# Output and mean-square matmuls of batches 1 to 7 on four quadrants of the TensorE array, with the order of work retuned

## The chip, the core and the metric

One core of a Trainium2 chip. The metric is device microseconds of one execution. Executions vary here by several per cent: a run counts as slow when it is over 1.5% above the fastest of its kernel, and fast runs are compared with fast runs. All positions in time below come from profiled executions. The two kernels were profiled in fast runs (192.91 us before).

## The reference

Linear attention without a mask, a root-mean-square norm per head, then a mixture of experts in which each of the 8 batches goes to one expert as a whole:

```python
kv  = einsum('bhsd,bhse->bhde', k, v)              # 8 batches, 8 heads, 576 tokens, 64 per head
out = einsum('bhsd,bhde->bhse', q, kv)
x   = out / sqrt(mean(out*out, -1) + 1e-6) * g_norm     # heads side by side: 576 x 512
e   = argmax(x.mean(tokens) @ w_gate)              # one of 8 experts for a batch
y   = softmax_prob[e] * relu(x @ w1[e]) @ w2[e]    # 512 -> 1024 -> 512
```

A batch's expert is known only when its attention is done, so the load of its weights can only be issued after its gate.

## The kernel before

The whole program is one list of steps, `ORDER`. A step is the batch, a letter, a number, and `x` where the eviction goes to the other of the two eviction engines:

```python
# L load q/k/v   T transpose q   K  k^T v of all heads   O  kv^T q (a pair of heads)
# M mean square  X normalise     G  gate: 0 sums, 1 matmul + index, 2 exp on GpSimd, 3 value
# W load the expert's weights (0: w1, 1: w2)   D warm-up matmuls
# m expert units: 0-7 blocks of layer 1, 9-16 halves of layer 2, 8 the last 64 tokens
ORDER = ( ... "2Q0x 0D1 0G2x 1K0 2T0x 1O0 1O2 1M0 0G3 0m0 2T2 1O1 0m3x 3L0x 3L1 1M1 1X0x 1O3 0m4 "
  "0m5 1X1 1M2 1M3x 0m1 1X2 0m7 1X3x 1G0 3L2x 2T3x 2K0x 0m2 1G1 2O0 0m6x 1G2 2T1x 2O2 " ... )
```

Each engine works through its own part of the list in order. The parts that the argument touches:

```python
def s_o(b, c, h=None, x=False):                    # one pair of heads
    po = ... psum("a")                             # tag "a": two buffers for all attention steps
    for i in range(2):                             # two halves of 288 tokens, whole array
        nc.tensor.matmul(po[:, i, 0:HS], kvb[:, b % 2, c, :],   # kv of 2 heads, block-diagonal 128x128
                         s["qT"][:, c, i * HS:(i + 1) * HS], start=True, stop=True)
    nc.scalar.activation(part(s["sq", c], h), po, AF.Square)
    if b > 0:
        copy(x, o, po)                             # one 128x576 copy frees the buffer
def s_m(b, c, h=None):                             # the same with `ones`, block-diagonal 1/64
    ...
    nc.scalar.activation(part(s["rs", c], h), pm[...], AF.Abs_reciprocal_sqrt, bias=epsc)
def s_index(b, pg):                                # G1: the expert's index into a register of GpSimd
    evs.append(nc.values_load(ixs[0:1, b, 0:1], engines=(mybir.EngineType.Pool,), ...))
def s_w(b, i):                                     # old weights are first copied to this batch's slot
    nc.vector.tensor_copy(W[:, own, ...], W[:, ds(sv, 1), ...])
    nc.gpsimd.dma_start(W[:, own, :, fs], (moe_w1, moe_w2)[i][ds(ev, 1), :, fs] ..., cond=cond)
def load_qkv(b, ...):                              # all loads of q, k and v are issued by GpSimd too
    nc.gpsimd.dma_start(t[0:R, hs], src[b, hs]...)
```

GpSimd's instruction stream thus holds the load of q, k and v of later batches, the register load of each gate, the exponentials, and the weight loads: whatever waits there holds all that is listed behind it (a wait of 14.6 us below shows it).

Of the kernel before, what the change touches and what calls it, by code (L numbers as in the profile page):

```python
# [11 lines left out]
F32 = mybir.dt.float32  # L12
F16 = mybir.dt.float16
# [8 lines left out]



ORDER = (
    "0R1 0R2 0R0x 0K0x 0T0 0C0 0K1 0T1x 0O0x 2L0x 0C1 0D1 0O1x 0M0x 0K2x 0X0 0T2 0M1 0C2x "
    "0D1 0D1 0O2x 0T3 0X1x 0C3 0K3 0M2x 1T0 0O30x 0O31 0M30 2L2x 0D1 0D1 0D1 0X2 0M31 0D1 "
    "0X30 0D1 0D1 0X31x 0G1x 0W0x 2L1x 0P0x 0D1 1T1 1T2 1T3 0D1 0D1 0D1 0D1 0D1 0W1 0D1 "
    "2Q0x 0D1 0G2x 1K0 2T0x 1O0 1O2 1M0 0G3 0m0 2T2 1O1 0m3x 3L0x 3L1 1M1 1X0x 1O3 0m4 "
    "0m5 1X1 1M2 1M3x 0m1 1X2 0m7 1X3x 1G0 3L2x 2T3x 2K0x 0m2 1G1 2O0 0m6x 1G2 2T1x 2O2 "  # L30
    "4L0x 2O1 0m9 4L1 1G3x 2M0 0m10x 4L2x 3Q0 2M1x 0m8x 2X0 5L0x 2O3x 0m15 2M2x 0m13 2X1x "
    "1W0 2X2x 3T0x 0m14 5L2x 5L1x 2M3 3T1x 0m16x 2X3x 3K0 3T2x 2G0 0m11 3T3 3O0 1W1x "
    "0m12x 3O2 1m0 1m7 2G1x 1m2 2G2x 3M0x 4Q0 1m5 3X0x 4T0 1m1 3O1 2W0 1m6 1m4x 3M2x 1m3 "
    "3M1x 4K0x 2W1 1m11 4T1 6L0x 3O3x 2G3 1m9x 1m12 3X1x 4T3x 3X2 3M3 1m10x 4T2 1m13 4O0x "
    "1m15 4O2 1m16 4M0 3X3x 1m14x 3G0x 4O1x 5K0x 1m8 4M1 4X0 2m0 4O3 2m7 3G1x 2m4 5Q0 2m3 "
    "6L1x 2m5 5T0 4M3 3W0x 2m1 2m2 3G2x 4X1x 2m6 4M2 5T3 3G3 4X2 2m13x 2m14x 5T1 4X3x "
    "5O0x 2m9x 6L2x 3W1 2m10x 2m15x 2m16x 5O1 2m8x 4G0 5T2x 6Q0 5M0x 2m11x 2m12x 4G1 3m0 "
    "6T0x 7L0x 3m5 6T1x 4W0 3m7x 3m6 5X0x 6T2x 5M1 3m3x 3m4 5O3 4G2x 3m1x 4G3 6T3x 7L1 "
    "5X1x 3m2 5O2 6K0 3m8x 5M2x 3m13 5M3 3m11x 3m14x 5X2x 4W1x 5X3x 3m12 6O0 5G0x 7Q0 "
    "3m9x 3m10x 3m15 6M0 3m16x 7L2 4m0x 6O1x 4m1x 7T0x 4m2x 5G1x 7T2x 5G2x 4m7 4m5x 6O2 "  # L40
    "4m4 5W0x 6X0x 4m3 6O3 5G3 5W1x 4m6 6M2x 4m9x 4m10x 4m11x 6M1x 6M3x 4m12x 6X1x 6X2x "
    "7T1 4m8 7K0 6X3x 4m15 4m16 4m13x 7O0x 6G0 4m14 6G1x 5m0 5m4x 6W0 6G2x 5m7 7T3x 5m6 "
    "5m1x 7M0x 5m3 5m2 7X0x 5m5x 6G3x 7O1x 5m11 7O2 5m12x 6W1 5m15x 7M2x 5m16x 7M1 5m8 "
    "5m13x 7O3 5m9x 5m14x 7X1 5m10 7M3x 6m0 6m2 6m5 7X2x 6m3 7X3x 7G0x 7G1 6m6 6m7 6m1 "
    "6m4 7G2x 7G3x 6m11 7W0 6m12x 6m13x 6m14 6m9 6m10x 6m15 6m16 6m8 7m0 7m5 7m6 7W1x 7m2 "
    "7m3 7m1 7m7 7m4 7m13x 7m14x 7m15 7m16 7m11 7m12x 7m9x 7m10x 7m8x "
)


# [1 line left out]
def kernel(  # L51
# [11 lines left out]
    nc = tc.nc  # L63
# [16 lines left out]
    att = ctx.enter_context(tc.tile_pool(name="att", bufs=2))  # L80
    sm = ctx.enter_context(tc.tile_pool(name="sm", bufs=3))
    xp = ctx.enter_context(tc.tile_pool(name="xp", bufs=3))
    hp = ctx.enter_context(tc.tile_pool(name="hp", bufs=1))
    outp = ctx.enter_context(tc.tile_pool(name="outp", bufs=5))
    ps0 = tc.tile_pool(name="ps0", bufs=1, space=bass.MemoryType.PSUM)
    psp = [ps0.__enter__()]
# [42 lines left out]
    nc.vector.memset(ones, 0.0)  # L129
    nc.vector.memset(ones[0:64, 0:64], 1.0 / Dh)  # L130
    nc.vector.memset(ones[64:128, 64:128], 1.0 / Dh)
    epsc = const.tile([P, 1], F32)
    nc.vector.memset(epsc, EPS)
    mean = const.tile([P, P], F32)
# [17 lines left out]
    def s_qt(b, c, x=False):  # L152
        s = st[b]
        if "qT" not in s:
            s["qT"] = att.tile([P, NP, S], F16, tag="qT", name="qT")
        p32 = psum("t", 1, 1) if first[0] else psum("a")
        pt = p32.bitcast(F16)
        for j in range(NJ):
            if "qr" in s:
                nc.tensor.transpose(pt[:, 0, j * R:(j + 1) * R], s["qr"][0:R, c, j],  # L160
                                    ident[0:R, 0:R])
                continue
            for i in range(2):
                nc.tensor.transpose(pt[64 * i:64 * i + 64, 0, j * R:(j + 1) * R],
                                    kvq[b][0][0:R, 2 * c + i, j, :], ident[0:R, 0:R])
        s["pt", c] = pt
        if b > 0:
            s_tc(b, c, x)
# [15 lines left out]
    def s_kv(b, prs):  # L184
        kt, vt = kvq[b][1:3]
        kv = kvb[:, b % 2]
        p32 = psum("kv", 1, 1) if first[0] else psum("a")
        pk = p32[:, 0].rearrange("p (c e) -> p c e", c=NP)
        for c in prs:
            for j in range(NJ):  # L190
                for i in range(2):
                    nc.tensor.matmul(pk[64 * i:64 * i + 64, c, 64 * i:64 * i + 64],  # L192
                                     kt[0:R, 2 * c + i, j, :], vt[0:R, 2 * c + i, j, :],
                                     start=(j == 0), stop=(j == NJ - 1))
        cs = slice(prs[0], prs[-1] + 1)
        nc.vector.tensor_copy(kv[0:64, cs, 0:64], pk[0:64, cs, 0:64])
        nc.vector.tensor_copy(kv[64:128, cs, 64:128], pk[64:128, cs, 64:128])


    def part(t, h):  # L200
        return two(t) if h is None else two(t)[:, h:h + 1]

    def s_o(b, c, h=None, x=False):
        s = st[b]
        po = (psum("p", 1) if h == 1 else psum("m")) if first[0] else psum("a")
        for i in range(2) if h is None else (h,):
            nc.tensor.matmul(po[:, i, 0:HS], kvb[:, b % 2, c, :],  # L207
                             s["qT"][:, c, i * HS:(i + 1) * HS], start=True, stop=True)
        po = po[:, :, 0:HS] if h is None else po[:, h:h + 1, 0:HS]
        if not h:  # L210
            s["sq", c] = sm.tile([P, S], F16, tag="sq", name="sq")
        nc.scalar.activation(part(s["sq", c], h), po, AF.Square)  # L212
        if b > 0:
            o = two(sm.tile([P, S], F32, tag="o", name="o"))
            copy(x, o, po)
            po = o
        s["o", c, h] = po

    def s_m(b, c, h=None):
        s = st[b]  # L220
        pm = (psum("p", 1) if h is None else psum("tkv"[h:2 * h + 1], 1, 1)) if first[0] \
            else psum("a")
        for i in range(2) if h is None else (h,):
            nc.tensor.matmul(pm[:, i if h is None else 0, 0:HS], ones,  # L224
                             s["sq", c][:, i * HS:(i + 1) * HS], start=True, stop=True)
        if not h:
            s["rs", c] = sm.tile([P, S], F32, tag="rs", name="rs")
        nc.scalar.activation(part(s["rs", c], h), pm[:, 0:2 if h is None else 1, 0:HS],  # L228
                             AF.Abs_reciprocal_sqrt, bias=epsc)

    def s_x(b, c, h=None):
        s = st[b]
# [16 lines left out]

    def s_row():  # L250
        s = st[0]
        pg = psum("t", 1, 1)[0:1, 0, 0:E]
        for c in range(NP + 1):
            nc.tensor.matmul(pg, s["pl"][:, c:c + 1], wg[:, min(c, NP - 1)], start=(c == 0),
                             stop=(c == NP))
        s["pg"] = pg
        s_index(0, pg)

    def s_index(b, pg):
        n = pg.shape[0]  # L260
        mx = sm.tile([P, 8], F32, tag="mx", name="mx")
        nc.vector.max(mx[0:n], pg)
        nc.vector.max_index(ixs[0:n, b], mx[0:n], pg)
        evs.append(nc.values_load(
            ixs[0:1, b, 0:1], engines=(mybir.EngineType.Pool,), min_val=0, max_val=E - 1,
            skip_runtime_bounds_check_because="it is the index of the largest of E values"))
        return mx

    def s_dl(b, mx, pg):
# [32 lines left out]
    def s_w(b, i):  # L302
# [2 lines left out]
        cond = None  # L305
        if b > 0:
            if b > 1 and i == 0:
                st[b]["sv"] = nc.values_load(
                    st[b]["src"][0:1, 0:1], engines=(mybir.EngineType.DVE,), min_val=0,
                    max_val=NW - 1,  # L310
                    skip_runtime_bounds_check_because="it is one of two numbers of slots")
            sv = st[b].get("sv", 0)
            for h in range(2):
                n = W.shape[2] // 2
# [53 lines left out]
    def m_2(b, t, fcs, x=False):  # L368
# [7 lines left out]
        if t == 4:  # L376
# [6 lines left out]
            if last:  # L383
                ot = outp.tile([P, D // 2], F32, tag="ot4", name="ot4")
                scaled(x, ot, po[:, 0, 0:D // 2], b)
                for i in range(2):
                    eng = nc.scalar if i and b == B - 1 else nc.sync
                    eng.dma_start(ob[NJ - 1, R - 64:R, i * D // 2:(i + 1) * D // 2],
                                  ot[64 * i:64 * i + 64])
            return  # L390
        for fc in fcs:
            nc.tensor.matmul(po[:, 0, :], s["hT"][:, fc, t * P:(t + 1) * P], w2[:, fc, :],  # L392
# [28 lines left out]
    def emit(tok):  # L421
# [6 lines left out]
        if f == "m":  # L428
            unit(b, c, x)
        elif f == "D":  # L430
            warm(psum("kv", 1, 1) if first[0] else psum("a"), c)
        elif f == "R":
            cast_first(c)
        elif f == "P":
# [6 lines left out]
        elif f == "K":  # L441
            s_kv(b, [c] if b == 0 else range(NP))
        elif f == "C":
            s_tc(b, c)
        elif f == "G":
            if (b, c) == (0, 1):
                s_row()
# [2 lines left out]
        elif f == "Q":  # L450
            s_qr(b)
        elif f == "W":
            s_w(b, c)
        elif f == "L":
            load_qkv(b, 1, only=(c,))
        elif f == "T":
            s_qt(b, c, x)
        elif f == "O":
            s_o(b, c, h, x)
        else:  # L460
            dict(M=s_m, X=s_x)[f](b, c, h)

    for tok in ORDER.split():
        emit(tok)
# [30 lines left out]
```

## Time and profile before

| | before |
|---|---|
| median of 3 runs | 193.95 us (193.09 to 199.57) |
| TensorE busy | 170.8 us of a span of 191.0 |
| VectorE, ScalarE busy | 110.8 and 106.6 us |
| gate matmuls of batches 1, 2, 7 | 40.9, 58.0, 158.9 us |
| TensorE's last matmul ends | 187.05 us |

The page's main lines are in the prediction. Two more views are needed to compare with later. The first cuts TensorE's time into three stretches: from batch 1's k-v product to batch 2's gate, from there to batch 7's gate, and from there to TensorE's end. The columns of a table of stretches are the stretch, its length, then busy us and number of instructions of each engine, the mean clock granted to TensorE, the DMA share and GB/s.

```profile
26.75:58.00 31.25, 28.39 (x361) 20.07 (x361) 24.33 (x60) 22.35 (x36) 12.42 (x16) 1.00 1.30 213
58.00:158.90 100.90, 99.15 (x951) 67.81 (x951) 67.96 (x173) 64.02 (x101) 23.13 (x21) 1.00 1.17 218
158.90:187.05 28.15, 28.14 (x196) 17.00 (x194) 6.49 (x16) 11.90 (x18) 1.79 (x4) 1.00 0.37 95
```

TensorE is idle 2.9, 1.8 and 0.0 us in the three. The second view is TensorE's timeline of batch 1's attention, the first stretch of the kernel in which it has little else to do (start, length, line, operation, idle before it and who ended that):

```profile
26.75 0.95 PE L192 MATMUL ps_a<-vt,kt 96*64 96x64 f16 x48
...
28.66 0.82 PE L207 MATMUL ps_a<-qT,kvb 128*128 128x288 f16 x4 [0.35 <-DVE kvb L197]
30.61 0.40 PE L224 MATMUL ps_a<-sq,ones 128*128 128x288 f16 x2 [1.13 <-DVE o L179]
30.85 1.14 PE L352 MATMUL ps_m<-xT,W 128*128 128x288 f16 x8
...
40.94 0.28 PE L283 MATMUL ps_a<-ts,mean 128*128 128x8 f32 x2
```

From the product to the gate matmul it takes 14.19 us. The wait of 1.13 us for a copy is the longest; single pairs alternate with whole blocks of batch 0's layer 1 (L352).

### The profile page before, as it was taken

How to read it: one execution, taken by the hardware profiler on the slowest of the kernel's cores; microseconds unless marked ns; L12 is line 12 of the kernel's file. 1: busy time of each engine (PE TensorE's matmuls, PEld its weight loads, DVE VectorE, ACT ScalarE, POOL GpSimd, SP SyncE). 2: the span in 40 equal slices, each digit the busy share in tenths (PEclk: the TensorE clock that was granted, in tenths of full speed). 3: DMA queues.
4: the chain of work that ended last, by engine and by line, in shares of the span. 5: the costliest groups of instructions: out<-in, count | busy, mean ns of one | idle time of the engine just before them, and what ended most of it. 6: DMA issues, size and time to landing. Idle time of an engine off the chain costs nothing.

```text
span 191.0 us, 4338 instructions
## 1 busy us (share of the span) xinstructions
PE 170.8 (89%) x1691; PEld 113.0 (59%) x1691; DVE 110.8 (58%) x289; ACT 106.6 (56%) x168; POOL 50.4 (26%) x64
## 2 busy tenths in 40 slices
PE   0297787998999999899999999999999999999991
PEld 0253255775578755686568746867586568457541
DVE  2437374878878795585565785697754482332010
ACT  2146107767877767676666655675257656316512
POOL 7670098018305130016127020311022103000000
PEclk9999999999999999999999999999999999999998
DMA  5999999999999999999999999999999799062045
GB/s 157 194 202 205 201 200 189 206 208 201 229 239 246 205 207 240 255 228 203 221 259 235 205 217 243 264 188 170 239 260 187 154 158 210 18 160 76 0 113 134
DMA packets 37030, 36.91 MB, mean 193 GB/s; under 512 B 2706, under 2 KB 30354, under 8 KB 37010
## 3 DMA queue, kind: packets, MB, share of 16 engines
q0 software_dynamic: 29328, 26.30, 86.4%
q1 hardware_dynamic: 7394, 9.98, 18.2%
q10 hardware_dynamic: 288, 0.36, 0.7%
q8 instruction: 13, 0.21, 0.4%
q14 instruction: 7, 0.06, 0.1%
HBM read 61.88 MB, written 9.44 MB: 373 GB/s over the span
## 4 chain that ended last, share of the span: by engine, by line
PE 58%; DMA 23%; DVE 6%; issue 5%; ACT 4%; POOL 2%; POOLq 0%; DVEq 0%
PE ps_m L352 27%; PE ps_m L392 21%; DMA W<-in_moe_w_dram 12%; DMA qt<-in_q_dram 7%; DMA kt<-in_k_dram 4%; DVE o L179 3%; ACT sq L212 3%; PE ps_a L224 3%; PE ps_a L207 2%; PE ps_m L379 2%; PE ps_a L160 2%; DVE W L315 1%; PE ps_a L192 1%; POOL qt L103 1%; DVE qr L174 1%
## 5 line engine op out<-in xcount | busy, mean ns | idle before, releaser
L352 PE MATMUL ps_m<-xT,W 128*128 128x288 f16 x512 | 68.2, 286 | 1.2 <-DMA W<-in_moe_w_dram 1.2
L392 PE MATMUL ps_m<-W,hT 128*128 128x512 f16 x256 | 60.7, 379 | 0.0
L352 PEld LDWEIGHTS <-W 128*128 128x128 f16 x512 | 49.4, 98 | 13.9 <-DMA W<-in_moe_w_dram 1.6
L359 ACT ACTIVATE hT<-ps_m 128x576 f16<-128x576 f32 x51 | 33.2, 652 | 21.5 <-PE ps_m L352 21.3
L392 PEld LDWEIGHTS <-hT 128*128 128x128 f16 x256 | 24.2, 98 | 24.5 <-ACT hT L359 0.6
L326 POOL DMA_DIRECT2D W<-in_moe_w_dram x20 | 12.5, 628 | 74.6 <-DMA W<-in_moe_w_dram 16.5
L363 ACT ACTIVATE ot<-ps_m,gates 128x512 f32<-128x512 f32 (+1 forms) x26 | 17.0, 656 | 18.2 <-PE ps_m L392 12.9
L228 ACT ACTIVATE rs<-ps_a,epsc 128x576 f32<-128x576 f32 x28 | 20.5, 741 | 7.2 <-PE ps_a L224 6.7
L237 DVE SCALAR_TENSOR_TENSOR xT<-o,gcol,rs 128x576 f16<-128x576 f32 x28 | 22.4, 811 | 3.5 <-ACT rs L228 3.4
L212 ACT ACTIVATE sq<-ps_a 128x576 f16<-128x576 f32 x28 | 17.9, 648 | 10.6 <-PE ps_a L207 10.5
L179 DVE COPY o<-ps_a 128x576 f32<-128x576 f32 x20 | 15.0, 757 | 15.2 <-ACT sq L212 14.9
L277 POOL TENSOR_TENSOR lg<-base,dl 128x8 f32<-128x8 f32 x8 | 14.7, 1836 | 27.2 <-DVE src L296 17.7
L365 DVE TENSOR_SCALAR ot<-ps_m,gates 128x512 f32<-128x512 f32 (+1 forms) x14 | 9.4, 673 | 18.5 <-PE ps_m L392 16.6
L315 DVE COPY W<-W 128x2048 f16 (+1 forms) x28 | 19.3, 695 | 1.4 <-DVE src L296 0.5
L179 ACT COPY qT<-ps_a 128x576 f16<-128x576 f16 x15 | 9.5, 636 | 10.7 <-PE ps_a L160 10.7
L356 DVE TENSOR_SCALAR hT<-ps_m 128x576 f16<-128x576 f32 x13 | 9.8, 755 | 8.7 <-PE ps_m L352 8.7
L192 PEld LDWEIGHTS <-kt 96*64 96x64 f16 x384 | 7.5, 116 | 9.9 <-ACT kt L179 5.8
L224 PE MATMUL ps_a<-sq,ones 128*128 128x288 f16 x56 | 11.1, 286 | 2.1 <-DVE o L179 2.0
L207 PE MATMUL ps_a<-qT,kvb 128*128 128x288 f16 x56 | 11.3, 286 | 1.2 <-DVE o L179 0.8
L103 POOL DMA_DIRECT2D kt<-in_k_dram x10 | 7.5, 750 | 12.7 <-PE ps_m L352 12.4
L224 PEld LDWEIGHTS <-ones 128*128 128x128 f16 x64 | 6.0, 99 | 7.9 <-issue 3.2
L160 PEld LDWEIGHTS <-qr 96*128 96x128 f16 x144 | 8.7, 98 | 2.7 <-issue 0.4
(75 smaller groups left out, 138.1 us busy)
## 6 DMA issues: line engine op xcount, KB each, us to landing
W<-in_moe_w_dram POOLq DMA_DIRECT2D x14, 1024.0 KB, 14.1
out_dram<-ot SPq DMA_DIRECT2D x24, 192.0 KB, 5.7
qt<-in_q_dram POOLq DMA_DIRECT2D x7, 576.0 KB, 14.6
kt<-in_k_dram POOLq DMA_DIRECT2D x7, 576.0 KB, 10.4
vt<-in_v_dram POOLq DMA_DIRECT2D x7, 576.0 KB, 16.1
out_dram<-ot SPq DMA_DIRECT2D x39, 64.0 KB, 5.6
out_dram<-ot SPq DMA_DIRECT2D x16, 128.0 KB, 5.2
W<-in_moe_w_dram POOLq DMA_DIRECT2D x4, 256.0 KB
```

Of the source, the lines that this page charges most:

```text
L179: nc.scalar.copy(out, in_) if x else nc.vector.tensor_copy(out, in_)
L207: nc.tensor.matmul(po[:, i, 0:HS], kvb[:, b % 2, c, :], s["qT"][:, c, i * HS:(i + 1) * HS], start=True, stop=True)
L212: nc.scalar.activation(part(s["sq", c], h), po, AF.Square)
L224: nc.tensor.matmul(pm[:, i if h is None else 0, 0:HS], ones, s["sq", c][:, i * HS:(i + 1) * HS], start=True, stop=True)
L228: nc.scalar.activation(part(s["rs", c], h), pm[:, 0:2 if h is None else 1, 0:HS], AF.Abs_reciprocal_sqrt, bias=epsc)
L237: nc.vector.scalar_tensor_tensor(out=part(s["xT"][:, c, :], h), in0=s["o", c, h], scalar=gcol, in1=part(s["rs", c], h), op0=ALU.mult, op1= ...
L277: nc.gpsimd.tensor_tensor(lg, base, st[b]["dl"], ALU.pow)
L315: nc.vector.tensor_copy(W[:, own, h * n:(h + 1) * n], W[:, ds(sv, 1), h * n:(h + 1) * n].rearrange("p o c f -> p (o c) f"))
L352: nc.tensor.matmul(ph[:, i, 0:HS], w1[:, c, fb * P:(fb + 1) * P], s["xT"][:, c, i * HS:(i + 1) * HS], start=(c == 0), stop=(c == 3))
L359: nc.scalar.activation(two(s["hT"][:, fb, :]), ph[:, :, 0:HS], AF.Relu)
L363: nc.scalar.activation(out, in_, AF.Copy, scale=gates[:, b:b + 1])
L392: nc.tensor.matmul(po[:, 0, :], s["hT"][:, fc, t * P:(t + 1) * P], w2[:, fc, :], start=(fc == 0), stop=(fc == 7))
```

## The change

The block-diagonal operands are half zeros, so half of the array's work is wasted. The change puts four 64x64 matmuls of two pairs on the four quadrants at once. The second half of the tokens comes out with its two heads swapped, so the copy has to swap it back in three pieces. The order was searched anew for this, and with it came a second hidden-layer buffer, other buffers in the first phase, fewer warm-ups and another queue for the last store. Cut to its core:

```diff
 ORDER = (                                          # all of it new; around batch 1's attention:
+    "0D1 0M31 2L1x 1T0x 0X30x 0X31 1T2 0G1x 0P0 0D1 1T3 1T1 0W0x 1K0 1O0x 3L0 1Y0 0G2x "
+    "1Y1x 1M0 2Q0 1X0x 2T0 1O2 1Y3x 1Y2 1X1x 0m0x 2T2x 2T3 3L2 0W1 1M2x 0m4 0G3 1X2x 2K0 "
+    "2T1x 1X3 1G0 0m5 4L0 2O0x 2Y0 0m7 0m3x 1G1 3L1 2Y1x 3Q0 0m2 4L1x 2M0x 4L2 0m1x 3T0x "
-    hp = ctx.enter_context(tc.tile_pool(name="hp", bufs=1))
+    hp = ctx.enter_context(tc.tile_pool(name="hp", bufs=2))
+    ones4 = const.tile([P, P], F16)                # all 1/64
     # kv of batches 1 to 7: written twice, beside each other, in place of block-diagonal
+    nc.vector.tensor_copy(kv[r].rearrange("p c (i e) -> p c i e", i=2),
+                          pk[r, :, r].unsqueeze(2).to_broadcast([64, NP, 2, Dh]))
+    def quads(c, outs, lhs, rhs):
+        for n, rows in ((0, 0), (1, 1), (0, 1), (1, 0)):
+            r = slice(64 * rows, 64 * rows + 64)
+            for i in range(2):
+                e = slice(64 * (rows ^ i), 64 * (rows ^ i) + 64)
+                nc.tensor.matmul(outs[n][e, i, 0:HS], lhs(c + n)[r, e],
+                                 rhs(c + n)[r, i * HS:(i + 1) * HS], start=True, stop=True)
+    def s_o2(b, c):                                # two pairs: takes both "a" buffers
+        po = [psum("a") for _ in range(2)]
+        quads(c, po, lambda n: kvb[:, b % 2, n, :], lambda n: s["qT"][:, n, :])
+        ...                                        # two squares on ScalarE
+    def s_y(b, c, x):                              # step Y: the copy, now by itself
+        copy(x, o[:, 0], po[:, 0, 0:HS])
+        copy(x, o[0:64, 1], po[64:128, 1, 0:HS])
+        copy(x, o[64:128, 1], po[0:64, 1, 0:HS])
     # (cut: s_m2 likewise with ones4; first-phase psum tags; the two register loads; the last store)
```

## The prediction

> **What bounds the kernel now.** I read four views. First the page's busy shares, slices and DMA rate:
>
> ```profile
> PE 170.8 (89%) x1691; PEld 113.0 (59%) x1691; DVE 110.8 (58%) x289; ACT 106.6 (56%) x168; POOL 50.4 (26%) x64
> ...
> PE   0297787998999999899999999999999999999991
> ...
> DMA  5999999999999999999999999999999799062045
> ```
>
> TensorE is full from about 30 us to 187 us, but the 16 DMA engines are full from about 8 us to about 150 us too. Two resources are near their bound at once, so the next question is how hard DMA is at its bound. A table of two stretches gives 220 GB/s written over 120 us:
>
> ```profile
> 8.00:128.00 120.00, 110.84 (x1205) 74.72 (x1206) 82.25 (x217) 75.26 (x121) 37.84 (x41) 1.00 1.26 220
> 128.00:160.00 32.00, 31.69 (x280) 21.24 (x278) 19.91 (x52) 17.54 (x27) 4.25 (x4) 1.00 1.05 195
> ```
>
> Nearly all loads read f32 and write f16, so a written byte stands for two read. Split by queue and counted by the wider side, the packets of each 8 us stretch from 8 to 128 us give 0.387 to 0.411 MB/us, whatever the mix: a constant of about 0.40. Loads are served in order of issue; there is always one waiting. So until about 130 us a load lands when all bytes ahead of it have passed, at 0.40 MB/us.
>
> Third, the costly groups, for TensorE's work and what evicts it:
>
> ```profile
> L207 PE MATMUL ps_a<-qT,kvb 128*128 128x288 f16 x56 | 11.3, 286 | 1.2 <-DVE o L179 0.8 <-DVE kvb L197 0.4
> L224 PE MATMUL ps_a<-sq,ones 128*128 128x288 f16 x56 | 11.1, 286 | 2.1 <-DVE o L179 2.0
> L179 DVE COPY o<-ps_a 128x576 f32<-128x576 f32 x20 | 15.0, 757 | 15.2 <-ACT sq L212 14.9
> L179 ACT COPY o<-ps_a 128x576 f32<-128x576 f32 x8 | 5.1, 635 | 0.0
> ```
>
> The 286 ns are pipelined latency; start to start such a matmul takes 122 ns. Fourth, the chain in order of time, for how the two resources meet:
>
> ```profile
> 65.45 12.98 DMA W<-in_moe_w_dram
> 78.43 0.05 issue
> 78.47 1.15 PE ps_m L352 x8
> ...
> 117.42 0.98 PE ps_m L352 x8
> ...
> 126.92 10.18 DMA W<-in_moe_w_dram
> 137.11 0.05 issue
> 137.16 3.12 PE ps_m L352 x24
> ...
> 186.04 1.01 PE ps_m L379 x16
> 187.05 0.03 issue
> ```
>
> TensorE meets weights of batch 2 at 78.4 us and of batch 5 at 137.1 us just as they land. The rest is TensorE work in one row to 187.05 us, then 3.9 us of last eviction and store. So the end is set by: landing of a weight, plus TensorE work ordered after its first use.
>
> **What the Trainium skill says.** "TensorEngine Tiling (Array Packing)", Key Properties: a change of tiling mode drains TensorE. The trace agrees: a 128x512 matmul is followed by the next after 216 ns, but by the first 128x64 one (L379) after 309, so 93 ns to enter; on the way back the last 106 ns pair takes 205, so 99 ns to leave. "TensorE: Matmul & The Clock Gate", Part 3: matmuls on different tiles start about 4 ns apart. The trace agrees for two column halves (L379: 3 to 4 ns, then 106); no run yet shows four quadrants. "TensorEngine Tiling", PSUM Bottleneck: tiling does not speed up PSUM eviction. "Perfetto Trace Analysis", Engine Utilization, puts the 16 DMA engines at about 435 GB/s in all; the 0.40 MB/us (400 GB/s) measured here is 92% of that, so I take it as a ceiling.
>
> **The change, part by part.**
>
> *Quadrant matmuls.* For batches 1 to 7, 14 pairs of pairs, each with an output and a mean-square step: 28 calls. Before, a call's work is 4 matmuls by 122 ns = 490 ns. After: 8 matmuls of 64x64 in two sets of four, 2 x 122 = 245 ns if four do run at once, plus 93 + 99 ns of drains, since nearly every call stands between 128-wide work: 437 ns. Saving 53 ns x 28 = 1.5 us, not the 6.9 us that 28 x 245 promises. In the order of work I find five calls beside a 128x64 block or another call's mode, worth at most 0.5 us more.
>
> *Eviction.* The swapped token half forces three copies in place of one: 28 x (128x288 and twice 64x288). From ACT's 128x512 and 128x256 evictions (689 and 474 ns) comes 0.84 ns per column, so 635 - 288 x 0.84 = 393 ns; from DVE's 750 and 482 comes 1.05, so 757 - 302 = 455 ns. With 14 pairs on each engine: 14 x 3 x (0.393 + 0.455) = 35.6 us against 15.0 + 5.1 = 20.1. The doubled kvb adds 14 x 256 columns x 1.05 ns = 3.8 us. Sum +19 us over two engines that have some 160 us free between them: off the path on average. But each output or mean call now takes both "a" buffers and frees the second only after two squares and copies, 0.35 + 1.3 + 1.2 = 2.9 us; the order puts two or three MoE units (0.87 to 0.99 us) between, so waits of some tenths remain.
>
> *Warm-ups.* 17 become 10: 7 x 0.22 = 1.5 us, all before 30 us, where TensorE idles anyway. Worth nothing.
>
> *Second hT buffer, new order.* These move the DMA meeting points. I give each unit its start-to-start time (first layer 8 x 0.123 = 0.985 us, second 4 x 0.216 = 0.866, last block 0.99, transposes of a pair 0.26, kv product 0.88, pair step 0.245, gate 0.12) and sum along the order. Check on before: from batch 4's first unit on there are 32 x 0.985 + 32 x 0.866 + 4 x 0.99 + 5.8 of attention = 68.9 us, and the chain has 187.05 - 117.42 = 69.6. After: from that same unit on, 32 first-layer and 40 second-layer units, 5 last blocks, 7 quadrant calls, 4 transposes, kv, 3 gates: 31.5 + 34.6 + 4.95 + 3.1 + 1.0 + 0.9 + 0.4 = 76.4 us. The second layer of batch 3 has moved behind it, attention has moved ahead.
>
> When can that unit start? Its W1 is loaded behind exactly the same set of other loads in both orders (all of batches 0 to 6 but the rest of k and v of 7, and weights of 0, 2 and 3; batch 1 repeats batch 0's expert and is skipped). In before it landed at 116.0 us by its semaphore, with about 4.5 MB of outputs stored by then; after, only three batches are stored, 3.5 MB. So it lands 1.0 / 0.40 = 2.4 us sooner, at 113.6. TensorE's end: 113.6 + 76.4 + 0.7 (the check's shortfall) = 190.7, against 187.05. The same sum at other points: first unit of batch 2, about 76 + 110.3 = 186.3; of batch 3, about 101.5 + 85.5 = 187; of batch 5, 132 + 53.3 = 185. So batch 4's weight is the worst, and TensorE should idle some 6 us before it, spread over such points. Attention savings before it go into waiting.
>
> **The rivals.** (a) TensorE bound, drains cheap: if quadrants ran with no drain and DMA did not hold, 6.9 us off: 187 us. For it: TensorE's 89%. Against: the drains measured above, and DMA's constant rate. (b) DMA holds, as worked out: PE end 190.7, +3.6, so about 197. With four-way overlap and free drains the tail is 75.1 in place of 76.4: 196. (c) Eviction becomes the bound: quadrant calls wait for the "a" buffers and MoE units for ACT. Against: (110.8 + 106.6 + 19) over two spans is some 61% each. For: the "a" waits on L179 are already the largest idle of L224 (2.0 us). Each 0.1 us of wait on the 7 calls of the last stretch is 0.7 us: up to 199. (d) The four quadrants do not overlap: 8 x 122 + 192 per call, 28 x 0.73 us = 20 us: over 210; I give it 3%. (e) The new order hides loads better than my sum says, since it was surely searched for gain: 190 to 192.
>
> **Range and chances.** Before's fast runs are 193.09 and 193.95. Working (b) gives +3.6 us on these, 197.1. I draw it back a little for (e), to 196.5, which is +1.5%. Range 192.5 to 199.5. Faster by over 2%: 0.08 (needs (a) and no DMA hold); within 2%: 0.53; slower: 0.39, as (b) with a little of (c) is already past 2%.
>
> **What would show it.** Right: DMA full and at 0.40 MB/us to about 130 us; TensorE idle of several us between 45 and 115, ended by DMA of W or of k and v; batch 4's first L352 unit starting at 113 to 115 us; some 76 us of TensorE from there; matmuls of a quadrant call in fours, with about 90 to 100 ns extra on either side; copies to o near 0.4 us, three per pair. Wrong: TensorE without idle and a shorter tail; batch 4's unit before 111 us; drains under 50 ns; or ACT and DVE as the releasers of most of TensorE's idle.

## The result, and the profile after

The changed kernel took 209.33 us in the median of 4 runs (207.31 to 212.11), the kernel before, in the runs taken with it and earlier, 195.77 (193.09 to 199.57). The ratio of the fast runs is 1.0782, with a 95% interval of 1.0626 to 1.0939. A ratio is always the mean time of one kernel's fast runs over that of the other's of the same rounds, so it is not quite the ratio of the medians. The change is slower by 7.8%; the prediction said 196.5 us, with 192.5 to 199.5 as its range.

The busy line and slices of the changed kernel's page, to be set beside those in the prediction:

```profile
PE 179.8 (87%) x1796; PEld 109.9 (53%) x1796; DVE 118.2 (57%) x308; ACT 118.6 (57%) x209; POOL 49.8 (24%) x64
...
PE   1678737898999899999898979999949999999990
...
PEclk9985855569999999999999999999988999999997
...
DMA  6999999996999989999999999999999843002554
```

No engine has become a bound: VectorE and ScalarE stand at 57%. But there are holes now in DMA's row, and TensorE's clock is at half for much of the stretch from the fourth to the ninth slice. The three stretches (from batch 1's product to gate 2, to gate 7, to TensorE's end) show where the time went:

```profile
24.66:67.10 42.44, 36.04 (x445) 23.13 (x444) 28.85 (x74) 27.14 (x51) 14.67 (x18) 0.76 1.21 190
67.10:169.60 102.50, 95.29 (x935) 57.88 (x933) 71.58 (x181) 66.95 (x119) 21.75 (x21) 0.98 1.09 203
169.60:203.12 33.52, 33.51 (x243) 21.20 (x241) 7.98 (x18) 13.66 (x21) 2.10 (x4) 1.00 0.32 86
```

TensorE's end moved from 187.05 to 203.12 us, by 16.1. The first stretch is 11.2 us longer (42.44 against 31.25), the second 1.6, the third 5.4; the first stretch began 2.1 us sooner. These four make 16.1.

What each stretch had to do can be counted from the list, with the durations that the prediction used (0.985 us for a block of layer 1, 0.866 for half a step of layer 2, 0.245 for a pair on the whole array, 0.464 for a quadrant call as measured below, and so on). That is a count of mine, not a view:

| stretch | work before | length before | work after | length after |
|---|---|---|---|---|
| batch 1's product to gate 2 | 26.9 us | 31.25 | 27.0 us | 42.4 |
| gate 2 to gate 7 | 97.9 us | 100.9 | 91.4 us | 102.5 |
| behind gate 7 | 27.7 us | 28.15 | 33.3 us | 33.5 |

So the first stretch has the same work and takes 11 us more. The two tables of stretches split these: TensorE is busy 36.04 us there in place of 28.39, for the same work, and idle 6.4 us in place of 2.9. About 7.7 of the 11.2 us are thus work done more slowly, at a mean granted clock of 0.76, and 3.5 are waits. The second has 6.5 us less work and takes no less time. The third is longer because the list puts 36 units behind gate 7 where there were 30.

TensorE's timeline of batch 1's attention shows what fills the first stretch:

```profile
24.66 1.48 PE L195 MATMUL ps_a<-vt,kt 96*64 96x64 f16 x48 [0.35 <-DVE qT L182]
26.92 0.45 PE L220 MATMUL ps_a<-qT,kvb 64*64 64x288 f16 x2 [0.78 <-DVE kvb L204]
27.64 0.69 PE L220 MATMUL ps_a<-qT,kvb 64*64 64x288 f16 x6 [0.28 <-DVE kvb L204]
30.64 0.56 PE L371 MATMUL ps_a<-row,mean 1*128 1x8 f32 x2 [2.31 <-DVE o L182]
31.14 1.28 PE L220 MATMUL ps_a<-sq,ones 64*64 64x288 f16 x8
...
35.10 2.10 PE L391 MATMUL ps_m<-xT,W 128*128 128x288 f16 x8
...
39.84 2.10 PE L391 MATMUL ps_m<-xT,W 128*128 128x288 f16 x8
...
48.41 0.36 PE L324 MATMUL ps_a<-ts,mean 128*128 128x8 f32 x2 [0.36 <-DVE o L182]
```

The first product of two pairs waits for two casts of the doubled kv, one behind the other. It takes both "a" buffers, and TensorE's next step, a small matmul of batch 0's gate, waits 2.31 us until squares and copies of a whole pair are done. Only two blocks of batch 0 (L391) stand before 43 us, and each takes 2.10 us where the kernel before took 1.14: TensorE ran at half speed, by its clock record from 24.7 to 45.2 us. Batch 1's gate comes after 23.75 us in place of 14.19.

The lateness then reaches the loads. GpSimd's waits from 24 to 75 us (who waited for whom, us in total, times, longest):

```profile
POOL kt L104 <- DVE qr L177: 14.6, 1, 14.6
POOL W L365 <- DVE qT L182: 11.2, 1, 11.2
POOL W L365 <- DVE W L354: 11.2, 1, 11.2
```

The 11.2 us in front of L365 that end at 24.7 us are no effect of the change: the kernel before has a wait of 10.9 us there, to 24.05. The other two are new in their length. From 36 to 50.5 us GpSimd issued nothing: the load of batch 3's k stood in its stream at the place of batch 1's gate. DMA ran out of work, as the DMA share (next to last column) of two windows says:

```profile
48.00:56.00 8.00, 7.42 (x67) 4.44 (x67) 6.76 (x19) 6.83 (x14) 4.32 (x5) 1.00 0.77 108
...
72.00:76.00 4.00, 3.55 (x26) 1.35 (x25) 2.93 (x7) 2.89 (x6) 3.72 (x4) 1.00 0.66 91
```

Before, 72 to 76 us had a share of 1.11 and 239 GB/s. Last, the chain in order of time (start, length, what) for the weight that the prediction singled out, batch 4's:

```profile
121.51 0.77 DVE hT L395
122.28 0.04 issue
122.32 2.12 PE ps_m L391 x16
...
135.90 16.84 DMA W<-in_moe_w_dram
...
154.10 0.76 DVE ot L404
154.86 0.04 issue
154.90 1.92 PE ps_m L418 x16
```

By its semaphore this weight landed at 122.1 us, having been issued at 110.9; before it was issued at 101.5 and landed at 116.0. The chain doesn't name this landing at 122.3 us, but an eviction by VectorE (L395) that ended at 122.28: two waits end there within 0.2 us. TensorE had been busy until 120.95, so it was idle for 1.4 us only; the lateness had come before. A second wait is seen at 154.90: VectorE's in-order stream stood at a weight copy for a landing at 152.7 us, so the eviction that TensorE needed (L404) came late, for 2.7 us.

### The profile page after: what moved, and what is told of

It reads as the page before. It is cut to its first block, busy times and chain, and to the rows that moved or that the text cites.

```text
span 207.9 us, 4625 instructions
## 1 busy us (share of the span) xinstructions
PE 179.8 (87%) x1796; PEld 109.9 (53%) x1796; DVE 118.2 (57%) x308; ACT 118.6 (57%) x209; POOL 49.8 (24%) x64
## 4 chain that ended last, share of the span: by engine, by line
PE 47%; DMA 26%; DVE 9%; issue 6%; ACT 6%; POOL 3%; DVEq 0%; POOLq 0%
DMA W<-in_moe_w_dram 23%; PE ps_m L391 18%; PE ps_m L430 16%; DMA vt<-in_v_dram 3%; PE ps_m L418 3%; PE ps_a L220 3%; DVE o L182 3%; PE ps_a L195 2%; PE ps_a L163 2%; DVE W L354 2%; DVE kvb L204 2%; ACT sq L229 1%; ACT rs L247 1%; POOL qt L104 1%; PE ps_s L269 1%
## 5 line engine op out<-in xcount | busy, mean ns | idle before, releaser
L391 PE MATMUL ps_m<-xT,W 128*128 128x288 f16 x512 | 71.6, 294 | 2.1 <-DVE hT L395 1.4
L391 PEld LDWEIGHTS <-W 128*128 128x128 f16 x512 | 49.8, 101 | 19.2 <-issue 4.2
L365 POOL DMA_DIRECT2D W<-in_moe_w_dram x20 | 12.5, 626 | 95.3 <-DVE W L354 23.5
L402 ACT ACTIVATE ot<-ps_m,gates 128x512 f32<-128x512 f32 (+1 forms) x22 | 14.3, 649 | 25.0 <-PE ps_m L430 16.4
L404 DVE TENSOR_SCALAR ot<-ps_m,gates 128x512 f32<-128x512 f32 (+1 forms) x18 | 12.4, 688 | 25.8 <-PE ps_m L430 23.5
L182 DVE COPY o<-ps_a 64x288 f32<-64x288 f32 (+1 forms) x42 | 19.1, 455 | 11.3 <-ACT sq L229 10.8
L247 ACT ACTIVATE rs<-ps_a,epsc 128x576 f32<-128x576 f32 x28 | 19.2, 737 | 9.1 <-PE ps_a L220 9.1
L280 DVE SCALAR_TENSOR_TENSOR xT<-o,gcol,rs 128x576 f16<-128x576 f32 x28 | 22.2, 815 | 3.2 <-ACT rs L247 3.0
L182 ACT COPY o<-ps_a 64x288 f32<-64x288 f32 (+1 forms) x42 | 16.7, 398 | 0.3
L182 ACT COPY qT<-ps_a 128x576 f16<-128x576 f16 x20 | 12.6, 638 | 6.5 <-PE ps_a L163 6.5
L395 DVE TENSOR_SCALAR hT<-ps_m 128x576 f16<-128x576 f32 x13 | 9.8, 754 | 6.9 <-PE ps_m L391 6.8
L163 PE MATMUL ps_a<-ident,qr 96*128 96x96 f16 x144 | 10.9, 218 | 1.8 <-ACT rs L247 1.0
L204 DVE CAST kvb<-ps_a 64x512 f16<-64x512 f32 x14 | 9.6, 687 | 4.3 <-PE ps_a L195 4.2
L418 PE MATMUL ps_m<-W,hT 128*64 128x256 f16 x128 | 9.2, 293 | 2.7 <-DVE ot L404 2.7
```

What stands on the lines that cost most here:

```text
L163: nc.tensor.transpose(pt[:, 0, j * R:(j + 1) * R], s["qr"][0:R, c, j], ident[0:R, 0:R])
L182: nc.scalar.copy(out, in_) if x else nc.vector.tensor_copy(out, in_)
L247: nc.scalar.activation(two(s["rs", c + n]), pm[n][:, :, 0:HS], AF.Abs_reciprocal_sqrt, bias=epsc)
L280: nc.vector.scalar_tensor_tensor(out=part(s["xT"][:, c, :], h), in0=s["o", c, h], scalar=gcol, in1=part(s["rs", c], h), op0=ALU.mult, op1= ...
L391: nc.tensor.matmul(ph[:, i, 0:HS], w1[:, c, fb * P:(fb + 1) * P], s["xT"][:, c, i * HS:(i + 1) * HS], start=(c == 0), stop=(c == 3))
L402: nc.scalar.activation(out, in_, AF.Copy, scale=gates[:, b:b + 1])
```

## The experiments

Fifteen kernels ran. In short, with times from the profile of each; "first" is from batch 1's product to gate 2, "middle" from gate 2 to gate 7:

| kernel | fast runs over before | product to gate 1 | first | middle |
|---|---|---|---|---|
| before | 1 | 14.2 us | 31.3 | 100.9 |
| after | 1.0782 | 23.8 | 42.4 | 102.5 |
| order_alone | 1.0448 | 17.6 | 36.5 | 101.5 |
| three_copies | 1.0613 | 19.4 | 38.0 | 99.2 |
| plain_b1 | 1.0468 | 18.6 | 37.3 | 101.2 |
| delay_b1 | 1.0557 | 24.1 | 41.1 | 100.1 |
| hoist | 1.0582 | 22.8 | 41.5 | 98.6 |
| early_w | 1.0222 | 14.2 | 31.2 | 103.0 |
| gate1_v1, gate1_v2 | 0.9957, 1.0069 | 12.3, 14.7 | 32.8, 36.1 | 100.1, 99.8 |
| b1_before | 1.0813 | 14.2 | 38.1 | 104.2 |
| b1_cover | 1.0776 | 16.8 | 39.3 | 102.5 |
| b1_cover_plain | 1.0503 | 15.0 | 36.4 | 99.3 |
| warm2, warm3 | none, 1.0767 | 24.0, 22.2 | 42.7, 40.9 | 102.5, 102.0 |

quads_alone and warm, told below, are left out of the table. The profiles of order_alone, hoist, gate1_v2, b1_cover, warm3, quads_alone and warm fell in runs that count as slow (1.6 to 1.9% over their fastest), so their stretches may be a few us too long in all; what is said of times rests on the ratios of fast runs and their 95% intervals.

The theory with which I began: batch 1's attention has become slow, since the doubled casts, the three copies and the shared buffers lie open there, and the loop gate, load, weight, next gate carries this to the end. The rivals: the order itself, the clock, and quadrant calls that cost everywhere.

**The order without quadrants, and the quadrants without the order.** The first run is the changed kernel with whole-array matmuls, a single cast and one copy; the second is the order before, with quadrants put in and pairs joined.

```diff
 # order_alone: quads(c, po, ...) becomes
+        for n in range(2):
+            for i in range(2):
+                nc.tensor.matmul(po[n][:, i, 0:HS], kvb[:, b % 2, c + n, :],
+                                 s["qT"][:, c + n, i * HS:(i + 1) * HS], start=True, stop=True)
 # quads_alone: before, with s_o2, s_y, s_m2 of the change in the places of its O and M steps
```

> The changed kernel's order of work, buffers and first phase, but output and mean-square matmuls of batches 1 to 7 on the whole array as before: 4 matmuls of 128x128 a call, kvb not doubled, one copy of 128x576 in place of three. Theory A (the new order: loads stand behind the gates in GpSimd's queue, DMA runs dry, batch 4's weight lands 8.5 us later than worked out): stays slow, 203 to 209 us. Theory B (the quadrants themselves: both buffers held through three copies, so gates come late and the order only suffers from it): back to 194 to 198. Theory C (fewer warm-ups, TensorE at half clock from 12 to 44 us): stays at 207 to 210.

> The kernel before with its own order of loads, weights, MoE units and its first phase, but with quadrant matmuls, doubled kvb and three copies for batches 1 to 7; pairs are joined at the first of them, with two MoE units between the steps so that the buffers come free. Theory A: 193 to 197, since quadrants cost 464 ns a call against 490 (93 to enter, 371 to the next matmul), some 0.7 us saved in all, and the copies lie beside other work. Theory B: 201 to 208.

The order without quadrants took 202.0 to 203.4 us in fast runs, ratio 1.0448 (1.0356 to 1.0539). That is just under the range of Theory A. The quadrants in the old order took 225.45 in the median, ratio 1.1604. The latter says little of quadrants as such: the places that I chose for the joined steps left TensorE waiting 7.1 us for copies. It does say that quadrant calls dropped at these places into an order made for single pairs cost 16%. The former says that more than half of the loss, about 8.7 us of 194.5, comes with the new order, joined pairs and buffers, with no quadrant at work.

**Loads ahead of the gate.** Six loads that stood behind batch 1's gate in GpSimd's stream were moved ahead of it.

```diff
 # hoist: after, behind 0m3x and ahead of 1G1
+ 3L1 4L1x 4L2 5L0 5L1x 5L2x
```

> The changed kernel with six loads (k of batch 3, k and v of 4, q, k, v of 5) moved in GpSimd's queue ahead of the gate of batch 1, so that DMA is fed from 48 to 52 us, where it ran dry. Theory A: 202 to 206 (3.7 us of lost DMA time in that stretch come back in part; the later dry stretches at 72 to 77 and from 120 on stay). Theory B or C: some of it too, since this tells only whether dry DMA carries to the end; if it stays within 1 us of 208, dry DMA there is not on the path.

It took 204.34 and 205.78 us in fast runs, ratio 1.0582 (1.0458 to 1.0706, which overlaps with the change's interval). DMA was busy through the old hole, and the hole moved to 66 to 74 us, where the share was 0.68: by then GpSimd stood before batch 2's weights. Feeding DMA early seems to be worth part of the loss (2.0% by the ratios); most of it stays.

**Batch 1 alone on the whole array, and the copies alone.** The first keeps the changed kernel with quadrants from batch 2 on. The second adds only the split of the copy to order_alone.

```diff
 # plain_b1
+        if b == 1:
+            whole(c, po, lambda n: kvb[:, 1, n, :], lambda n: s["qT"][:, n, :])   # one cast, one copy
+        else:
             quads(c, po, ...)
 # three_copies: order_alone with
-        copy(x, o, po[:, :, 0:HS])
+        copy(x, o[:, 0], po[:, 0, 0:HS])
+        copy(x, o[0:64, 1], po[0:64, 1, 0:HS])
+        copy(x, o[64:128, 1], po[64:128, 1, 0:HS])
```

> The changed kernel with batch 1 alone back on the whole array (4 matmuls of 128x128 a call, one copy, kvb not doubled); batches 2 to 7 keep the quadrants. Theory D (the quadrants' two held buffers, long kv cast and three copies make batch 1's attention 6 us longer, while TensorE has nothing else to do, and every later gate and weight carries that lateness): batch 1's gate about 5 to 6 us sooner, 48.4 to 43, and the time 202 to 204. Rival E (each batch pays its own part of the quadrants): 206 to 208.

> The run with the new order and whole-array matmuls, with its single copy of 128x576 split into 128x288 and two of 64x288 on the same engine, nothing else. If the eviction is what the quadrants cost: 205 to 208 (that run: 202.7 median), batch 1's gate 2 us or more later. If it is the kv cast, the drains or the matmuls: within 1 us of 202.7.

plain_b1 took 202.85 to 204.71 us fast, ratio 1.0468 (1.0358 to 1.0578): to take the quadrants out of one batch of seven won back 6 us (1.0782 less 1.0468 is 3.1% of 194.5). Its gate 1 came 3.6 us sooner (44.8), not the 5 to 6 expected. The quadrants of the other six batches then cost 0.002 of it, nothing that can be resolved: the two intervals leave room for 1.4% either way. three_copies took 202.87 to 205.49 fast, ratio 1.0613: splitting the copies alone costs about 3 us (1.6% of 194.5, with 1.4% of uncertainty), so they may be about half of what the quadrants cost, though both eviction engines are idle for some 40% of the span.

**Is lateness carried?** In the kernel before, VectorE was held by eleven memsets of an unused tile ahead of batch 1's cast.

```diff
 # delay_b1: before, in s_kv
+        for _ in range(11 if b == 1 else 0):
+            nc.vector.memset(idle, 0.0)
         nc.vector.tensor_copy(kv[0:64, cs, 0:64], pk[0:64, cs, 0:64])
```

> The kernel before with 11 memsets of 128x576 on DVE, an estimated 6 us, put just ahead of batch 1's kv cast, so that its gate comes about 6 us late; nothing else is changed. Theory D: nothing later takes the lateness up, +5 to +6 us, 199 to 200. Rival: DMA and TensorE catch up in the later stages, under +2.5 us, 194 to 196.5.

The memsets took 7.8 us from first to last, gaps included, rather than the 6 that I had sized. Gates 1 to 7 came later by 10.9, 10.9, 9.8, 9.8, 10.0, 10.5 and 10.1 us, TensorE's end by 10.4; of that about 1 us is a later start of that profile. Ratio 1.0557. Lateness at batch 1 is hardly caught up by anything behind it (0.8 us in the middle stretch). All four of its runs were fast.

**Weights moved right behind their gate**, to see whether the loop before can be shortened from that side.

```diff
 # early_w: before; for batches 2 to 6 the first weight load right behind the gate
- 2G1x ... 3O1 2W0 ...
+ 2G1x 2W0 ... 3O1 ...
```

> The kernel before with the first weight load of batches 2 to 6 (and the copies ahead of it) moved right behind that batch's gate. If the landing of batch 5's weight at 137.1 us sets the end, it lands up to 4 us sooner; the next points (batches 2 and 3, 185.3 and 185.6 by my sum) leave 0.5 to 1.5 us: 192.3 to 193.5 for fast runs. If the copies on DVE now stand in front of evictions: same or slower, 194 to 196.

It took 195.98 to 198.6 us fast, ratio 1.0222 (1.0128 to 1.0317): slower than before, and slower than either branch of the expectation. The copy that belongs to each weight load now stands earlier in VectorE's stream too. At 62.6 and 85.9 us TensorE waits 1.17 and 0.72 us for a copy of q (L177) that VectorE does right behind such weight copies, waits that the kernel before doesn't have. That fits as a reason for a part; no run tested it.

**An earlier gate 1 in the kernel before.** If gate 1 set all, earlier would help.

```diff
 # gate1_v1: before
- 0m4 0m5 1X1 1M2 1M3x 0m1 1X2 0m7 1X3x 1G0 3L2x 2T3x 2K0x 0m2 1G1
+ 0m4 1X1 1M2 1M3x 0m5 1X2 0m1 1X3x 3L2x 1G0 1G1 0m7 2T3x 2K0x 0m2
 # gate1_v2: 0m0 and 0m3 moved back as well
```

> The kernel before with four units of batch 0's expert work moved behind batch 1's attention products, so that batch 1's gate comes earlier and nothing else changes. Theory (the time of batch 1's gate is carried through all later batches and into the end): gate matmul at 38.7 to 39.5 us against 40.9, every later gate earlier by the same, and 191 to 192.5 us fast. Rival (TensorE's own work is what sets the end of the kernel before, a gate that comes earlier only meets a full TensorE): 0 to 0.5 us sooner, or later.

> As the run before, with two further units of batch 0's first layer moved behind batch 1's attention. Theory (batch 1's gate sets all): gate at 38 to 39 us, 191 to 192.5 us fast, provided the moved units are not missed where TensorE waits for the attention's copies. Rival (TensorE bound): within 0.5 us of the kernel before, or slower, as the stretch between 30 and 40 us then has waits that nothing fills.

Ratios 0.9957 (0.9865 to 1.0049) and 1.0069 (0.9975 to 1.0164): both the same as before. In the first, the gate came 1.85 us sooner after batch 1's product (12.34 us against 14.19), and gate 2 nevertheless 1.5 us later (32.8 against 31.25). The theory as I had put it fell here in one half: late is carried, early was not in this order. The units that were moved away from batch 1 have to stand somewhere before gate 2, and they did.

**Batch 1 as in the kernel before, all the rest as changed.** This was meant as the proof.

```diff
 # b1_before: ORDER = that of before up to 1G1, then what is left of the changed order;
 #            first-phase buffers, kv, O and M of batches 0 and 1 as before
 # b1_cover: the same, with 0m5 0m1 0m7 0m2 left beside batch 2's attention as in the change
 # b1_cover_plain: b1_cover with the whole array for every batch
```

> The changed kernel with everything up to batch 1's gate as in the kernel before (its order, its buffers of the first phase, batch 1's attention a pair of heads at a time on the whole array); all that stands behind it, the quadrants of batches 2 to 7 and the new order included, is as changed. Theory (the 7.5 us by which batch 1's gate is later are carried in full; what lies behind it costs 5 to 8 us more by itself): gate matmul of batch 1 at 41 to 42 us, batch 7's at 161.5 to 163.5, time 200.5 to 203 us fast. Rival 1 (the lateness of batch 1 only hides other waits, so removing it wins little): 205.5 us or more, with the later gates catching up to those of the changed kernel. Rival 2 (all of the loss is batch 1's, the later order and the quadrants are harmless): 196 to 198 us.

> As the run with batch 1's old first phase, but the units of batch 0 that stand beside batch 2's attention in the changed kernel (second to seventh block of the first layer) stay there in place of being done ahead of batch 1's gate. If an early first gate is carried through as long as the next batch's attention has cover: gate 1 at 40 to 42.5 us, gate 2 at 59 to 62.5, batch 7's at 161 to 164, time 200.5 to 204 us fast. If the later order holds the gates back whatever the first one does: gate 2 at 64 us or later and 206 us or more.

> As b1_cover with the whole array for every batch, so that no quadrant is left and only the later order and the buffers differ from the kernel before. Theory: about 1 us under b1_cover, so 199.5 to 203 us, all of which above 195.5 is the later order's own. Rival (the quadrants of batches 2 to 7 cost more as soon as batch 1 does not hide it): 3 us or more under b1_cover.

My expectation missed. b1_before had gate 1 at 42.0 us in place of 48.4, and took 209.6 to 211.7 us (ratio 1.0813; all six runs count as fast, at a granted clock of 0.946 to 0.965). Gate 2 came at 65.9 us against 67.1: 5.2 of the 6.4 us had been lost again. TensorE's timeline just behind gate 1 has one line that says how:

```profile
46.39 0.65 PE L220 MATMUL ps_a<-sq,ones 64*64 64x288 f16 x8 [2.23 <-DVE o L182]
```

It is the wait of the changed kernel's batch 1, 2.31 us there, now in batch 2: with batch 0's units used up early, its quadrant calls lie open. Behind it TensorE ran at half speed again: the next eight matmuls of batch 0 (48.99 us) took 2.12 us. b1_cover was to mend that and did not: its first stretch was 39.3 us, gate 2 came at 69.4, its ratio was 1.0776, and half of its runs, the profiled one too, were slow. Without any quadrant the first stretch was 36.4 us and the ratio 1.0503, the rival's branch of that expectation:

```profile
27.80:64.20 36.40, 32.08 (x408) 23.26 (x407) 24.31 (x63) 24.56 (x40) 12.77 (x16) 0.91 1.30 206
64.20:163.40 99.20, 95.27 (x858) 63.17 (x855) 64.02 (x162) 61.62 (x101) 21.70 (x21) 0.98 1.14 211
163.40:196.99 33.59, 33.59 (x243) 21.25 (x242) 7.98 (x18) 13.68 (x21) 2.09 (x4) 1.00 0.32 86
```

So here the quadrants of batches 2 to 7 cost 2.7% (some 5 us), where beside plain_b1 no cost could be resolved. Their price is not fixed to a batch. By the two waits above it falls due where attention has too little work beside it. And gate 1 alone does not decide: with no quadrant anywhere the first stretch is 36.4 and 36.5 us in two kernels whose gate 1 differs by 2.6 us in this measure, against 31.3 before. Nor does a shorter first stretch alone: that of b1_before is 4.4 us shorter than the change's, but it starts 3.2 us later and its middle stretch is 1.7 us longer.

**The clock.** TensorE ran at half speed from 24.7 to 45.2 us in the changed kernel's profile. Three kernels put warm-up matmuls there.

```diff
 # warm: 0D2 for 0D1, 0D4 and 16-matmul groups; they read kvb and so waited for its cast
 # warm2: the same on an operand long there:  1K0 0E6 1O0x 3L0 1Y0 0G2x 1Y1x 0E8 1M0 0E3
 # warm3: groups where TensorE waits anyway:  1K0 0E5 1O0x 0E9 3L0 1Y0 0G2x 1Y1x 1M0 0E2
```

> The changed kernel with more warm-up matmuls on TensorE: twice as many in each place up to the first gate, 4 after it, and 16 in the waits of batch 1's attention. Theory C: granted clock above 0.98 and 198 to 203 us. Theory A or B: clock up, time within 2 us of 208; one of the four runs of the changed kernel had a clock of 0.997 and took 209.13 us, which speaks for this.

> The changed kernel with its warm-up matmuls on an operand that is long there (batch 0's q, not the cast that batch 1's products wait for) and more of them, right ahead of and between batch 1's attention products. If the half clock between 33 and 45 us is part of why batch 1's attention takes 23.75 us: gate matmul 2 to 3 us sooner (45 to 46.5 us) and 205 to 206.5 us fast. If the lateness is waits for copies and buffers alone: gate within 0.7 us of 48.4, time 208 to 209.5 us.

> As the second warm-up run, with the eight matmuls (now nine) ahead of the row gate, where TensorE waits 2.3 us for copies in the changed kernel, five behind batch 1's kv product and two behind its first mean-square step, so that none stands where the path is. If half clock is a part of the 23.75 us from batch 1's kv product to its gate: 20.5 to 22 us, and the time 205.5 to 207.5 us fast (the gate 2 to 3 us sooner is carried to gate 2). If waits for buffers and copies alone set it: 23 to 24 us and 207.5 to 209.5.

In the first, warm, four warm-ups waited 1.48 us for the cast themselves and six stood in the path (2.74 us, at half speed); its only fast run took 206.63 us. As a run it told nothing, but its profile, of a slow run, is at full speed from 37 us to gate 1:

```profile
38.40 1.14 PE L394 MATMUL ps_m<-xT,W 128*128 128x288 f16 x8
...
48.80 0.36 PE L327 MATMUL ps_a<-ts,mean 128*128 128x8 f32 x2 [0.32 <-DVE o L185]
```

The same steps, from batch 0's first block to gate 1, took 10.4 us there and 13.3 in the changed kernel (35.10 to 48.41), where most of them ran at half speed. What was won there the warm-ups had cost before. warm2 kept blocks at full speed up to 40 us, but eight warm-ups stood in the path (3.4 us, at half speed) and gate 1 was at 48.5 us as before; its two fast runs took 206.56 and 209.65 us. warm3 shortened the way to gate 1 by 1.6 us (22.2 against 23.75), then TensorE fell back to half speed at 35 us; two lines show both sides of it:

```profile
29.51 2.12 PE L476 MATMUL ps_m<-qT,ones 128*128 128x512 f16 x9
...
35.89 2.10 PE L394 MATMUL ps_m<-xT,W 128*128 128x288 f16 x8
```

Nine warm-ups fill a wait (0.22 us each, full speed), and eight matmuls of batch 0 take 2.10 us six us later. Fast runs took 206.28 to 208.99 us, ratio 1.0767 (1.0699 to 1.0835), which can't be told from the change's 1.0782. Half speed thus has a share in the lateness. From batch 1's product to batch 0's first block, warm3 took 9.2 us where the change took 10.4; with the 2.9 us of warm behind it that makes some 4 of the 9.6 us to gate 1, an estimate from two profiles. How much it is in a whole run stays open, as no run kept full speed through to gate 1, and why the clock fell is not shown.

None of the fifteen beats the kernel before.

## Why the prediction was wrong

**The step that failed.** The prediction let batch 4's first weight land at 113.6 us, because "Loads are served in order of issue; there is always one waiting". It landed at 122.1. Everything ahead of it did not pass at 0.40 MB/us: counted as the prediction did, the rate was 0.22 from 48 to 56 us and 0.27 from 72 to 80. These two stretches alone fall short by 2.5 MB, which is 6.2 of the 8.5 us. The bytes were the same; the issues were not. Loads stand in GpSimd's stream behind gates, and a gate stands behind attention, which the sum had left out by letting "Attention savings before it go into waiting". The prediction's own sum is then off by 8.7 us at its first term (TensorE could start that unit at 122.3 in place of 113.6) and by 3.7 at its second: 80.8 us of TensorE from there against 76.4 + 0.7, of which 2.7 are the one wait for L404; half speed behind that wait adds some 1.5 (L418 took 1.92 us there, 1.06 at 136.7). Together 12.4 us: 190.7 became 203.1. The picture of TensorE idle before that weight is wrong as well: it expected several us of idle between 45 and 115 us, ended by DMA, and the one wait that a landing ended there took 0.7 us. At the unit itself it was 1.4 us, with VectorE's eviction the last to end, so a landing at 113.6 alone would not have let it start then. (A slip of 0.1 us: 1.0 / 0.40 is 2.5, not 2.4.)

**The term mis-sized behind it.** "waits of some tenths remain", it said of the calls that take both buffers. In batch 1, where there is little to put between, it was 9.6 us more from product to gate. By the runs, the order with joined pairs and other buffers brings 3.4 us of these by itself (17.6 against 14.2), splitting the copies a further 1.8 (three_copies), and the rest, 4.4, is what remains for the quadrants' doubled cast and all else that they bring. These are differences of single profiles, each with half speed in its own part of the way. The sum has no term for the clock at all: of the 11.2 us more in the first stretch, 7.7 are TensorE busy with the same work.

**Right.** Four quadrants do run at once: in a warm call the eight matmuls start at 0, 3, 7, 10 and 147, 150, 153, 157 ns, and the next whole-array one at 371. With the 93 ns on entry a call takes 464 ns against the 437 worked out and the 490 before, as the second four start 147 ns behind the first and not 122: 0.7 us are saved over 28 calls, where 1.5 were predicted. The copies came out as predicted, 455 ns on VectorE and 398 on ScalarE against 455 and 393, and so did the doubled cast (687 ns against 427 before). Evictions added busy time and no bound. What fewer warm-ups cost is not shown: with twice as many of them, in warm and warm2, the clock fell at 29.9 and 29.8 us in place of 24.7. The direction of the middle value was right too, though the chances leaned to "within 2%" (0.53 against 0.39). One of the signs that the prediction had named for "wrong" turned up, VectorE and ScalarE as releasers of most of TensorE's idle time in the first stretch; and of its signs for "right", DMA full to about 130 us, the unit at 113 to 115 us and some 76 us from there did not.

**The rivals.** (a), TensorE as the bound, is out for the changed kernel: 6.5 us less work between gates 2 and 7 brought no time. (b), DMA as the hold, was right in kind, yet DMA's rate is not what holds. The loop from gate to load to gate is the reading that fits: the middle stretch is 98.6 to 104.2 us in all the kernels of the table, with 91 to 98 us of work in it by count. No run took that loop apart, and the one that shortened it on the side of the load, early_w, was slower. (c), eviction, is what TensorE's waits show, but in one stretch and not on average, and waits are the smaller part there. (d) is out, and (e) is the reverse of what was found: the new order does more behind gate 7, 33.3 us in place of 27.7, as if gate 7 were to come earlier, and it does not.

**The account of the 15 us**, by ratios on 194.5 us: 8.7 with the order, joined pairs and buffers; about 6 with the quadrants in batch 1, half of which the split copies can make by themselves; none to be seen, within 1.4%, with those of batches 2 to 7 as they stand. Within the first part, the profile of order_alone has 5.3 us in the first stretch and 5.4 behind gate 7, in a slow run, so more than the 8.7 in all; of the 5.3, 4.3 are TensorE busy, partly at half speed, and 1.0 are idle. Order, joined pairs and buffers were not tested one by one.

**Open.** Why the first stretch of the new order takes 36.4 us with the old batch 1 and no quadrant (b1_cover_plain): its TensorE is idle 4.3 us against 2.9, and some 6.5 us of it ran at half clock; which of the order's moves does it was not taken apart. The share of the half clock and its cause, as said above.

## What to carry to other kernels

Ask of every stretch what stands beside it: a step that takes two buffers and three copies in place of one cost nothing that could be resolved where expert work covered it, and some 6 us where attention stood alone. Read TensorE's busy time and clock beside its waits: here the same work took 36.0 us in place of 28.4. Where loads are issued behind results, a DMA that was always full before is no constant: carry the issue times through the loop in the estimate, since a lateness at its start reached the end nearly undiminished, while an earliness was not passed on. Saving 6.5 us of TensorE work in the stretch between the gates brought nothing here, and moving work behind the last gate added its whole length, 5.4 us.

## What the Trainium skill lacked or had wrong

- "TensorEngine Tiling (Array Packing)", Key Properties, says that a change of tiling mode drains TensorE, but not how long. Here it is 93 ns on entry and about 100 on leaving, so a call of eight 64x64 matmuls of 288 columns takes 464 ns against 490 for four on the whole array: nearly all of the gain goes into the drain.
- "TensorE: Matmul & The Clock Gate", section "Why this matters for your kernels", asks for no idle gaps over some 3 us. In warm3 TensorE fell to half clock at 35 us for about 10 us, though no wait from 26.7 us on was longer than 0.37 us; TensorE was busy for 2.29 of the 3.4 us before. So that rule alone does not keep the clock up. It is a gap of the rule and not of the page, which elsewhere tells of short idles between groups that bring half clock.
- No page says what it costs when loads stand in an engine's stream behind a register load of a gate; that engines take their work in order is said. Here it is 14.6 and 11.2 us of GpSimd, with DMA's share down to 0.66.
- The clock row of the profile can miss: in hoist its records begin at 45.8 us and the row shows full speed before that too, while eight matmuls of 288 columns took 2.10 us at 38.2 and 42.9 us, as at half speed. This is no gap: "TensorE: Matmul & The Clock Gate", Part 1, warns that the clock's trace events can be unreliable.
